# A planned attention and squared-relu kernel: a clock of transfers under way, and the values' maximum kept behind the relu passes of the second up product

## The chip, the core and the metric

The kernel runs on one core of a Trainium2 chip. The metric is device time in microseconds, the median of several executions; lower is better. The core has TensorE (PE in the profile; its weight loads are PEld), VectorE (DVE), ScalarE (ACT), GpSimd (POOL) and SyncE (SP). Each runs its own list of instructions in order and waits on semaphores for the others. Transfers are issued from the lists of POOL, SP and ACT.

## The reference

```python
# q: (8, 16, 384, 64); k, v: (8, 4, 384, 64); w_in: (1024, 2048); w_out: (2048, 1024)
k = np.repeat(k, 4, axis=1); v = np.repeat(v, 4, axis=1)
scores = np.matmul(q, k.transpose(0, 1, 3, 2)) / np.sqrt(64)
attn = np.exp(scores - np.max(scores, axis=-1, keepdims=True))
attn = attn / (np.sum(attn, axis=-1, keepdims=True) + 1e-09)
x = np.matmul(attn, v).transpose(0, 2, 1, 3).reshape(3072, 1024)
h = np.maximum(x @ w_in, 0.0)
return (h * h @ w_out).astype(np.float32)
```

Inputs and output are float32. Each of the 8 batches gives 384 rows of `x`.

## The kernel before

**Stages.** A batch `b` passes through loads of q, k and v (POOL queue, cast to bf16), transposes of k and q by DMA (SP queue; `turn_k_half`, `turn_q_dma`), scores on TensorE with the exponential on ScalarE (L476), the product with the values (`av_halves`, L533) with the division on VectorE (L546, L548), a transpose of the result into `xT` by DMA (`turn_o_dma`, L553), the up product with `w_in`, the relu and the square, and the down product with `w_out`, whose results are stored from the tiles `y_sb` (L1329).

**Up and down products.** For batches 0 and 1 the up product is done in quads (`quad`): four tiles of 128 columns in banks 4 to 7 of PSUM, in phases; VectorE takes the relu of a phase out of two banks (L642) before TensorE may fill them again. From batch 2 on, both products are of Strassen's kind: seven products of sums of quarters. The sums of the input are made on VectorE (`sums`, L676, a queue named `lazy`, whose last entry, L679, marks the batch as summed; only then is its up product offered). `strassen` puts units of the up product into the four banks of `order`, and the down products follow in the same banks. VectorE and ScalarE evict each down product into a y tile (L1114, L1115, L1121); for product 7 GpSimd adds two y tiles (L1153), and product 4 is then evicted into one of the tiles that this pass reads.

**Scales.** The kernel works in scaled 16-bit numbers. The largest value of `v` in a batch is reduced on VectorE (`top_of`, L691 and L693), spread over the partitions by TensorE (`top_spread`, L703, L707), and made into a unit (`v_unit`, L712) before attention of that batch may start. It waits in a queue `top_q`. In the second up product (batch 1) VectorE also scales `w_out` in place, pass by pass (`here2`, L1247), whenever its clock is near that of TensorE.

**Order of the work.** Nothing of the order is written out by hand. `Recorder` keeps a clock for every engine, with a cost for every operation. Two loops choose, step by step, the next piece for TensorE by the time at which its inputs are ready by these clocks; before each step `upkeep(now)` hands passes to the other engines from queues, by conditions on the clocks. `emit` then writes each engine's list with the waits. A change of a cost or a condition therefore moves the order of much that comes after it.

**Transfers.** From batch 2 on, `calm_at` decides whether a load or a transpose may be issued. It works from the number of TensorE instructions recorded so far: TensorE's instructions are fetched in blocks, and a block is taken as 128 matmuls with an offset `EDGE`. Where TensorE issues 18 or more matmuls per us, a transfer may start if the next edge is at least 1.5 us away and the last one 0.3 us past. `dma_at` keeps a gap of 2.0 us after a load and 3.5 us after a transpose. This applies to the loads and the transposes of k and q from batch 4 on, and to the transposes of attention's output in the second loop.

Of the kernel before, what the change touches and what calls it, by code (L numbers as in the profile page):

```python
# [21 lines left out]
class Recorder:  # L22


    ENGINES = ("tensor", "scalar", "vector", "gpsimd", "sync")
    IN_ORDER = ("tensor",)

    def __init__(self, nc):
        self.nc = nc
        self.ops = []  # L30
        self.writer = {}
        self.readers = {}
        self.dma_sems = {}
# [27 lines left out]
    def add(self, eng, fn, reads=(), writes=(), dma=None, cost=0.1, issue=0.1, shared=(), after=(), port=False):  # L61
# [19 lines left out]
        start = max([self.clock[eng]] + [self.ops[d]["end"] for d in need])  # L81
        if dma is not None:
# [7 lines left out]
            if shared and self.ring.get("gpsimd", 0.0) > begin:  # L90
# [76 lines left out]
def bass_gqa_attention__then__ffn_squared_relu_kernel(  # L167
# [17 lines left out]
    NKC = F // 128  # L185
# [1140 lines left out]
    def send(b, i3, c0, c1, yb, y0=0):  # L1326
        ysl = y_sb[yb][:, y0:y0 + c1 - c0]
        rows = out[b * S:(b + 1) * S, :].rearrange("(p j) f -> j p f", j=NJ)[i3]
        put = lambda: R.add("sync", lambda e: e.dma_start(rows[:, c0:c1], ysl),  # L1329
                            reads=[("y", yb)], writes=[("out", b, i3, c0)], dma=f"y{yb}" + "z" * (y0 > 0), cost=0.6)  # L1330
# [108 lines left out]
    def prepare(b):  # L1439
# [218 lines left out]
    o_wait = []  # L1658

    def turn_o_waiting():  # L1660
        while o_wait:
            b, g = o_wait.pop(0)
            turn_o_dma(b, g, tuple(pe_last))
            dma_at[0] = max(dma_at[0], R.clock["tensor"] + 3.5)
            x_done[b] += 2

    def upkeep(now):
        nonlocal loaded, queued, turned
        pe_last[0:1] = [len(R.ops) - 1 - next(i for i, o in enumerate(reversed(R.ops)) if o["eng"] == "tensor")]
        if o_wait and calm_at(now):  # L1670
            turn_o_waiting()
        if loaded + 1 < B and turned >= loaded and not turn_q and not load_pieces and not chores:
# [17 lines left out]
            else:  # L1690
# [3 lines left out]
                if n < LATE:  # L1694
                    load_pieces.append(([("v_st", 0)], lambda g: load_v(n, g)))
        if load_pieces and now >= dma_at[0] and calm_at(now) and R.when(writes=load_pieces[0][0], reads=(load_pieces[0] + ((),))[2], eng="none") + 2.0 <= now:
# [7 lines left out]
        stretch[0] = split and ff["b"] < SB or bool(ff["now"])  # L1704
        while chores and R.when(reads=chores[0][0], eng="none") + (chores[0] + (False, 0.0))[3 if len(chores[0]) > 3 else -1] <= now + margin and not (len(chores[0]) > 2 and chores[0][2] and (now < dma_at[0] or not calm_at(now))):
            chores.pop(0)[1]()
            if not chores and not halves:
                turned = queued
# [17 lines left out]
        if m_q and not spread_q and (not ff["now"] or R.clock["vector"] <= now) and not (wide_q and wide_q[0][0] <= m_q[0][0]) and R.clock["vector"] <= now + 0.6:  # L1726
            m_q.pop(0)[1]()
        if top_q and (not spread_q or queued >= LATE) and top_q[0][2]() and (ff["b"] < SB or not ff["now"] or queued >= LATE) and R.when(reads=top_q[0][0], eng="none") + (4 if queued < LATE else 0.0) <= now + margin:
            top_q.pop(0)[1]()
# [286 lines left out]
```

## Time and profile before

| | us |
|---|---|
| median of 3 runs | 399.15 (398.44 to 399.24) |
| the profiled execution | 397.95 |
| its span | 396.0 |
| TensorE busy | 388.1 (98%) |
| VectorE busy | 316.3 (80%) |
| ScalarE busy | 264.4 (67%) |
| GpSimd busy | 151.1 (38%) |

The granted clock of TensorE is 1.00 throughout. Roughly, by the instructions on TensorE: the opening and batches 0 and 1 up to 125 us; the up products of batches 2 to 7 from about 128, 168, 222, 259, 313 and 348 us, each followed by its down product; the last matmul ends at about 392.8 us and the last store lands at 395.6 us.

A row of the timeline gives start, duration, engine, line, operation, tiles written and read, shapes, count, and in brackets the idle time of the engine before it with what ended it. A row of waits gives who waited for whom, the total, how often, and the longest. A row of windows gives the stretch, its length, the busy time of PE, PEld, DVE, ACT and POOL, the clock, the share of DMA and GB/s. A row by line and tile gives the count, the shortest, median and longest duration in ns, and the first and last start. "q" behind an engine is its sequencer. Ends of matmuls are modelled.

### The profile page before, as it was taken

Reading aid. Unit: us, or ns where it says so; the run is one execution under the profiler, and the core shown is the slowest. Engines: PE = TensorE matmul, PEld = TensorE weight load, DVE = VectorE, ACT = ScalarE, POOL = GpSimd, SP = SyncE. Lnnn points to the kernel's source line nnn. Section 1 sums busy time; section 2 is a strip of 40 time slices with the busy share of each in tenths; the row PEclk is TensorE's granted clock in tenths of the full one; section 3 lists DMA queues with packets and bytes.
Section 4 is the critical chain, followed back from the end, with each engine's and each line's share of the span. In section 5 each row is a group of like instructions: output and inputs, shape, how many; then the busy total and the mean of one; then the engine's idle time right before and its main releaser. Section 6 shows DMA issues by size and latency. Waiting matters only on the chain.

```text
span 396.0 us, 15645 instructions
## 1 busy us (share of the span) xinstructions
PE 388.1 (98%) x7022; PEld 292.1 (74%) x7022; DVE 316.3 (80%) x654; ACT 264.4 (67%) x384; POOL 151.1 (38%) x173
## 2 busy tenths in 40 slices
PE   8999999999999999999999999999999999999996
PEld 5565764455655998499876899799974799789653
DVE  3689879899989998878997888878897688856642
ACT  6948999688556796578728587868725597426511
POOL 8656410056002565068413263066420145126111
PEclk9999999999999999999999999999999999999999
DMA  9999999995229936659469957484476221120022
GB/s 171 175 199 187 207 186 192 180 221 82 41 77 141 163 49 83 109 123 102 64 112 190 139 89 73 89 149 58 65 107 167 79 45 25 46 84 3 28 81 106
DMA packets 95634, 44.39 MB, mean 112 GB/s; under 512 B 75984, under 2 KB 89552, under 8 KB 95568
## 3 DMA queue, kind: packets, MB, share of 16 engines
q0 software_dynamic: 36672, 17.44, 35.4%
q1 hardware_dynamic: 58224, 25.47, 32.1%
q8 instruction: 55, 0.90, 0.9%
q10 hardware_dynamic: 672, 0.49, 0.4%
q14 instruction: 11, 0.09, 0.1%
HBM read 35.65 MB, written 12.58 MB: 122 GB/s over the span
## 4 chain that ended last, share of the span: by engine, by line
PE 87%; DVE 7%; DMA 3%; POOL 1%; issue 1%; ACT 0%; ACTq 0%; DVEq 0%
PE ps L963 30%; PE ps L921 27%; PE ps L629 7%; PE ps L466 7%; PE ps L533 7%; PE ps L1297 5%; DMA wx<-in_q_dram 2%; PE ps L492 2%; DVE hr L642 1%; PE ps L592 1%; DMA wx<-in_k_dram 1%; DVE w_out_sb L1247 1%; DVE y_sb L1121 1%; DVE w_out_sb L1259 1%; DVE s_all L676 0%
## 5 line engine op out<-in xcount | busy, mean ns | idle before, releaser
L476 ACT ACTIVATE expT<-ps 128x1024 bf16<-128x1024 f32 (+1 forms) x124 | 121.1, 1017 | 37.6 <-PE ps L466 37.2
L963 PE MATMUL ps<-w_out_sb,h2T 64*128 64x512 f16 x528 | 96.3, 376 | 0.0
L921 PE MATMUL ps<-xT,w_in_sb 64*128 64x192 f16 x1152 | 84.2, 243 | 0.4 <-DVE y_sb L1121 0.3
L921 PEld LDWEIGHTS ps<-xT,w_in_sb 64*128 64x128 f16 x1152 | 71.4, 94 | 3.4 <-DVE y_sb L1121 0.5
L818 POOL TENSOR_TENSOR h2T<-hr 128x384 f16<-128x384 f32 x56 | 45.4, 832 | 45.6 <-ACT hr L806 45.4
L963 PE MATMUL ps<-area,xT 64*128 64x512 f16 x288 | 55.3, 376 | 0.0
L963 PEld LDWEIGHTS ps<-w_out_sb,h2T 64*128 64x128 f16 (+1 forms) x528 | 38.5, 94 | 19.0 <-ACT h2T L814 0.5
L921 PE MATMUL ps<-s_all,wx 64*128 64x192 f16 x768 | 51.8, 243 | 0.0
L466 PE MATMUL ps<-qT,kT 64*128 64x256 bf16 (+2 forms) x336 | 50.3, 323 | 0.9 <-ACT expT L476 0.6
L806 ACT ACTIVATE hr<-hr,bits 128x384 f32<-128x384 f32 x71 | 41.9, 608 | 10.1 <-DVE hr L905 9.5
L921 PEld LDWEIGHTS ps<-s_all,wx 64*128 64x128 f16 x768 | 44.4, 94 | 0.7
L905 DVE TENSOR_TENSOR hr<-ps,hr 128x384 f32<-128x384 f32 x72 | 39.2, 554 | 6.3 <-PE ps L921 2.5
L533 PE MATMUL ps<-v_aug,expT 64*128 64x65 bf16 x1680 | 43.9, 190 | 0.1
L1121 DVE SCALAR_TENSOR_TENSOR y_sb<-ps,bits,y_sb 128x512 f32<-128x512 f32 (+2 forms) x38 | 27.1, 723 | 20.4 <-PE ps L963 9.6
L629 PE MATMUL ps<-xT,w_in_sb 64*128 64x384 bf16 x448 | 41.9, 323 | 1.0 <-DVE hr L642 0.9
L533 PEld LDWEIGHTS ps<-v_aug,expT 64*128 64x128 bf16 x1680 | 39.9, 94 | 1.4 <-PE ps L533 0.2
L1114 ACT ACTIVATE y_sb<-ps,bits 128x512 f32<-128x512 f32 x20 | 13.6, 687 | 35.4 <-PE ps L963 35.4
L963 PE MATMUL ps<-area,h2T 64*128 64x512 f16 x144 | 36.2, 376 | 0.0
L1153 POOL TENSOR_TENSOR y_sb<-y_sb 128x512 f32<-128x512 f32 x9 | 11.9, 1320 | 62.7 <-DVE y_sb L1121 62.7
L629 PEld LDWEIGHTS ps<-xT,w_in_sb 64*128 64x128 bf16 x448 | 21.9, 94 | 16.2 <-DVE hr L642 2.2
L921 PE MATMUL ps<-xT,wx 64*128 64x192 f16 x384 | 33.0, 243 | 0.2 <-DVE hr L905 0.2
L921 PE MATMUL ps<-s_all,w_in_sb 64*128 64x192 f16 x384 | 32.7, 242 | 0.0
(147 smaller groups left out, 748.5 us busy)
## 6 DMA issues: line engine op xcount, KB each, us to landing
out_dram<-y_sb SPq DMA_DIRECT2D x45, 256.0 KB, 2.5
w_in_sb<-in_moe_w_in_dram POOLq DMA_DIRECT2D x8, 512.0 KB, 15.2
w_out_sb<-in_moe_w_out_dram POOLq DMA_DIRECT2D x4, 1024.0 KB, 28.4
q_st<-in_q_dram POOLq DMA_DIRECT2D x19, 192.0 KB, 4.9
q_st<-in_q_dram POOLq DMA_DIRECT2D x4, 384.0 KB, 23.5
k_st<-in_k_dram POOLq DMA_DIRECT2D x6, 192.0 KB, 4.5
k_st<-in_v_dram POOLq DMA_DIRECT2D x5, 192.0 KB, 3.8
wx<-in_q_dram POOLq DMA_DIRECT2D x2, 384.0 KB, 9.1
```

The costliest lines, as they stand in the source:

```text
L466: mm = pe.matmul(ps[:, base + x, m * wide:(m + 1) * wide], kT[at(b)][64 * x:64 * x + 64, u, :], q_cols(b, u // NJ, x, c0, c0 + wide))
L476: R.add("scalar", lambda e: e.activation(dst, src, AF.Exp, scale=0.125), reads=keys, writes=[("expT", slot(b, u), t) for u, _, _ in pieces ...
L533: m = pe.matmul(ps[:, p[x], n * DP:n * DP + D + 1], w, v_aug[b % 2][r, g * NJ + j, 0:D + 1], start=(n + j + y == 0), stop=(n + j + y == 2 ...
L629: m = pe.matmul(bank(4 + xs[x])[:, 0:S], w_in_sb[r, kc, c * 128:(c + 1) * 128], xT[b % NXT][r, kc, :], start=(phase < 2 and kc == 0), stop ...
L806: R.add("scalar", lambda e, val=val, to=to: e.activation(val, val, AF.Relu, scale=to), reads=[("hr", r)] + by, writes=[("hr", r)], cost=0. ...
L818: n = R.add(eng, lambda e, dst=dst, two=two: e.tensor_tensor(dst, two, two, ALU.mult), reads=[("hr", r)], writes=keys, cost=0.77 if other ...
L905: R.add("vector", lambda e: e.tensor_tensor(hr[r][:, :], src, hr[r][:, :], ALU.add), reads=[("bank", at), ("hr", r)], writes=[("hr", r)], ...
L921: return lambda pe: pe.matmul(bank(at)[:, f * h:f * h + h], w[r, kc, c:c + 128], m[r, kc, :], start=(prod in (1, 5, 2) and y + f + kc == 0 ...
L963: return lambda pe: pe.matmul(bank(p.at)[:, 0:512], p.a(k, r), p.w(k, r), start=start, stop=stop, skip_group_check=True)
L1114: R.add(eng, lambda e: e.activation(y_sb[y], bank(at), AF.Copy, scale=gs[g]) if eng == "scalar" else e.tensor_scalar(y_sb[y], bank(at), gs ...
L1121: R.add("vector", lambda e: e.scalar_tensor_tensor(y_sb[z][:, c0:c1], bank(at)[:, c0:c1], gs[g], y_sb[y][:, c0:c1], ALU.mult, ALU.add), re ...
L1297: m = pe.matmul(bank(i)[:, 0:n], h2T[:, c, i3 * 128:(i3 + 1) * 128], w_out_sb[:, c, c0:c1], start=(c == 0), stop=(c == NFC - 1))
```

## The change

- A clock of transfers: every transfer that is recorded adds to `wire`, with a lag and a duration by kind. `calm_at` now asks, by kind, whether the transfers under way with the new one would be over within 6 us (where TensorE issues under 18 matmuls per us), or within 2 us past the next edge, or whether an edge is at most 0.3 us away and what is under way ends within 2 us.
- The gaps behind a load and a transpose become 0.5 us from batch 2 on, and the gap of 3.5 us behind the transpose of an attention output becomes 0.
- `shut`: from batch 2 on, a pass of `lazy` isn't handed to VectorE while, at the later of the two clocks, a GpSimd operation is under way in the plan with over 0.3 us left.
- `top_q` isn't served in the second up and down product (`ff["b"] == 1`) while VectorE's clock is over 0.3 us past TensorE's.
- The last batch's products use banks 0 to 3 in place of 4 to 7.
- The store of the second piece of the last tile (`y0` not 0) is issued from ScalarE's list in place of SyncE's.
- A bound in front of `add_sums` is written with one case more, of the same value.

```diff
+    WIRE = dict(turn_q=(1.6, 1.9), turn_o=(0.8, 1.3), turn_k=(1.3, 1.3), y=(1.8, 0.8))
...
+        self.wire = 0.0
...
             self.ring[q] = begin + cost
+            kind = dma.rstrip("0123456789z_")
+            lag, work = self.WIRE.get(kind, (2.2, 1.25))
+            self.wire = max(self.wire, start + lag) + work
...
-        put = lambda: R.add("sync", lambda e: e.dma_start(rows[:, c0:c1], ysl),
+        put = lambda: R.add("scalar" if y0 else "sync", lambda e: e.dma_start(rows[:, c0:c1], ysl),
...
-                dma_at[0] = R.clock["tensor"] + TURN_GAP
+                dma_at[0] = R.clock["tensor"] + (TURN_GAP if ff["b"] < SB else 0.5)
...
+            if b == B - 1:
+                order[:] = [0, 1, 2, 3]
             built[b] = strassen(b, ff["carry"])
...
-    def calm_at(now):
+    def calm_at(now, kind):
...
         rate = (n - m) / (now - t)
+        lag, work = R.WIRE.get(kind, (2.2, 1.25))
+        over = max(R.wire, now + lag) + work
         if rate < 18:
-            return True
+            return over <= now + 6.0
         left = (EDGE - n) % BLOCK / rate
-        return 1.5 <= left <= BLOCK / rate - 0.3
+        return (over <= now + left + 2.0 or left < 0.3 and R.wire <= now + 2.0) and left <= BLOCK / rate - 0.3
...
-            dma_at[0] = max(dma_at[0], R.clock["tensor"] + 3.5)
+            dma_at[0] = max(dma_at[0], R.clock["tensor"] + 0)
...
+    def shut(now):
+        t = max(now, R.clock["vector"])
+        return ff["b"] >= SB and any(a <= t < z - 0.3 for a, z in R.pool[-6:])
...
-            dma_at[0] = now + LOAD_GAP
+            dma_at[0] = now + (LOAD_GAP if ff["b"] < SB else 0.5)
...
-        while lazy and R.when(reads=lazy[0][0], eng="none") <= now + near and R.clock["vector"] <= now + near:
+        while lazy and R.when(reads=lazy[0][0], eng="none") <= now + near and R.clock["vector"] <= now + near and not shut(now):
             lazy.pop(0)[1]()
...
-        if top_q and (...) and R.when(reads=top_q[0][0], eng="none") + (4 if queued < LATE else 0.0) <= now + margin:
+        if top_q and (...) and R.when(reads=top_q[0][0], eng="none") + (4 if queued < LATE else 0.0) <= now + margin and not (ff["b"] == 1 and R.clock["vector"] > now + 0.3):
             top_q.pop(0)[1]()
...
-        if b and R.when(reads=[("xT", b % NXT, c) for c in range(NKC)], eng="none") + (3.3 if b > SB else 2.0) <= now + 0.3:
+        if b and R.when(reads=[("xT", b % NXT, c) for c in range(NKC)], eng="none") + (3.3 if b > SB + 1 else 3.3 if b > SB else 2.0) <= now + 0.3:
             add_sums(b)
```

The calls of `calm_at` pass the kind: `"turn_o"` for attention's output, `"q"` for loads, `"turn_q"` for the transposes of k and q.

More of the change, by code (lines that the diff above doesn't have):

```diff
@@ L1669, in upkeep @@
         pe_last[0:1] = [len(R.ops) - 1 - next(i for i, o in enumerate(reversed(R.ops)) if o["eng"] == "tensor")]
-        if o_wait and calm_at(now):
+        if o_wait and calm_at(now, "turn_o"):
             turn_o_waiting()
@@ L1695, in upkeep @@
                     load_pieces.append(([("v_st", 0)], lambda g: load_v(n, g)))
-        if load_pieces and now >= dma_at[0] and calm_at(now) and R.when(writes=load_pieces[0][0], reads=(load_pieces[0] + ((),))[2], eng="none") + 2.0 <= now:
+        if load_pieces and now >= dma_at[0] and calm_at(now, "q") and R.when(writes=load_pieces[0][0], reads=(load_pieces[0] + ((),))[2], eng="none") + 2.0 <= now:
             load_pieces.pop(0)[1](tuple(pe_last[0:1]))
-            dma_at[0] = now + LOAD_GAP
+            dma_at[0] = now + (LOAD_GAP if ff["b"] < SB else 0.5)
         if not chores and halves and (halves[0] - 1, NU - 1, 5) in scored and (halves[0] > LATE or x_done[halves[0] - 1] == NKC):
@@ L1704, in upkeep @@
         stretch[0] = split and ff["b"] < SB or bool(ff["now"])
-        while chores and R.when(reads=chores[0][0], eng="none") + (chores[0] + (False, 0.0))[3 if len(chores[0]) > 3 else -1] <= now + margin and not (len(chores[0]) > 2 and chores[0][2] and (now < dma_at[0] or not calm_at(now))):
+        while chores and R.when(reads=chores[0][0], eng="none") + (chores[0] + (False, 0.0))[3 if len(chores[0]) > 3 else -1] <= now + margin and not (len(chores[0]) > 2 and chores[0][2] and (now < dma_at[0] or not calm_at(now, "turn_q"))):
             chores.pop(0)[1]()
@@ L1727, in upkeep @@
             m_q.pop(0)[1]()
-        if top_q and (not spread_q or queued >= LATE) and top_q[0][2]() and (ff["b"] < SB or not ff["now"] or queued >= LATE) and R.when(reads=top_q[0][0], eng="none") + (4 if queued < LATE else 0.0) <= now + margin:
+        if top_q and (not spread_q or queued >= LATE) and top_q[0][2]() and (ff["b"] < SB or not ff["now"] or queued >= LATE) and R.when(reads=top_q[0][0], eng="none") + (4 if queued < LATE else 0.0) <= now + margin and not (ff["b"] == 1 and R.clock["vector"] > now + 0.3):
             top_q.pop(0)[1]()
```

## The prediction

> **What bounds the kernel now.** I read the page's busy shares and chain first, then TensorE's own waits, then the timeline around each wait, last the tail and the transfers.
>
> ```profile
> span 396.0 us, 15645 instructions
> PE 388.1 (98%) x7022; PEld 292.1 (74%) x7022; DVE 316.3 (80%) x654; ACT 264.4 (67%) x384; POOL 151.1 (38%) x173
> PE 87%; DVE 7%; DMA 3%; POOL 1%; issue 1%; ACT 0%; ACTq 0%; DVEq 0%
> PE ps L629 <- DVE hr L642: 0.9, 2, 0.7
> PE ps L963 <- DVE y_sb L1121: 0.6, 1, 0.6
> PE ps L466 <- ACT expT L476: 0.6, 3, 0.3
> PE ps L921 <- DVE y_sb L1121: 0.3, 1, 0.3
> ```
>
> TensorE is busy 98% of the span and is 87% of the chain, so only what makes TensorE wait, and the tail after its last matmul, can be won. Its waits (total, times, longest) are short and few: the four rows give 2.4 us, and VectorE, evicting late, is behind 1.8 of them. The 7% of VectorE in the chain are these places. So I go through the change by what it does to them.
>
> **The change, part by part.** *The values' maximum behind the relu passes (the new condition on `top_q` while `ff["b"] == 1`).* VectorE, then TensorE, at the place of the longest wait:
>
> ```profile
> 80.86 0.17 DVE L1244 RECIPROCAL bits<-bits 128x1 f32<-128x1 f32 x1
> 80.94 0.93 DVE L691 TENSOR_REDUCE bits<-area 128x1 f32<-128x768 bf16 x1
> 81.91 0.23 DVE L693 CAST top_w<-bits 128x128 bf16<-128x128 f32 x1
> 82.06 1.01 DVE L642 TENSOR_SCALAR hr<-ps 128x384 f32<-128x384 f32 x2
> 82.99 2.63 DVE L1247 TENSOR_SCALAR w_out_sb<-w_out_sb,bits 128x1024 f16<-128x1024 bf16 x5
> ...
> 80.71 0.65 PE L629 MATMUL ps<-xT,w_in_sb 64*128 64x384 bf16 x6
> 81.63 0.81 PE L629 MATMUL ps<-xT,w_in_sb 64*128 64x384 bf16 x8
> 83.13 0.34 PE L629 MATMUL ps<-xT,w_in_sb 64*128 64x384 bf16 x2 [0.68 <-DVE hr L642]
> ```
>
> The maximum and its cast (0.93 + 0.23 us) stand ahead of two relu passes. The phase whose banks they empty ended at 80.71 + 0.65 = 81.36. Without the maximum the pair would run from there to 81.36 + 1.01 = 82.37, and TensorE's other work lasts to 81.63 + 0.81 = 82.44. The whole wait goes: 0.68 us. On the chip VectorE has no gap between the passes up to here; the planner's VectorE clock, which follows the same passes, is then past `now + 0.3`, and the condition bites. The maximum isn't removed: it runs behind the pair, among the scale passes of L1247, which only have to be done before the down product from about 101 us. That is its cover: about 18 us. If it lands ahead of a later relu pair instead, it costs up to the same 0.68; range 0 to 0.68, taken 0.68, because the room of 2.63 us behind the pair holds its 1.16.
>
> *`shut`: no sum on VectorE while the plan has a GpSimd pass under way.* VectorE, GpSimd, TensorE in the down product of batch 5, then the groups of both operations:
>
> ```profile
> 295.96 0.54 DVE L676 TENSOR_TENSOR xT<-xT 128x768 f16<-128x768 f16 x1
> 296.42 1.62 DVE L676 TENSOR_TENSOR s_all<-xT,s_all 128x768 f16<-128x768 f16 x1
> 297.97 0.74 DVE L1121 SCALAR_TENSOR_TENSOR y_sb<-ps,bits,y_sb 128x512 f32<-128x512 f32 x1
> ...
> 296.12 1.51 POOL L1153 TENSOR_TENSOR y_sb<-y_sb 128x512 f32<-128x512 f32 x1 [2.83 <-DVE y_sb L1121]
> ...
> 298.76 0.39 PE L963 MATMUL ps<-w_out_sb,area 64*128 64x512 f16 x1 [0.63 <-DVE y_sb L1121]
> ...
> L676 DVE TENSOR_TENSOR s_all<-xT,s_all x6: 548/550/1621, 126.4 to 345.0; 128x768 f16<-128x768 f16 x6
> L1153 POOL TENSOR_TENSOR y_sb<-y_sb x9: 1256/1268/1507, 167.6 to 391.3; 128x512 f32<-128x512 f32 x9
> ```
>
> The sum takes 1.62 us beside the GpSimd pass and 0.55 in the median; the pass ends at 296.12 + 1.51 = 297.63, and the sum 0.4 us behind it. Moved away from the pass, the sum frees VectorE for 1.62 - 0.55 = 1.07 us.
>
> TensorE does not get that much. The eviction of L1121 at 297.97 writes the y tile that the GpSimd pass reads (product 7's `a3`, product 4's target), so it waits for that pass too: alone it would end at 296.12 + 1.27 = 297.39, the eviction at 298.13, TensorE would start at 298.18 and not 298.76. That is 0.58. Late next are the two sums, 0.54 + 0.55 us, which now stand between later evictions; their reader, the up product of batch 6, starts 15 us on. Bounds 0 (the sums make the next eviction late by as much) and 0.63 (the wait's row); taken 0.5, nearer the upper, since TensorE's other evictions here show no wait. For the other batches the guard delays a sum by less than one GpSimd pass, hidden by the same distance, but for one place (second rival).
>
> *Banks 0 to 3 for the last batch (`order[:]`).* At its start TensorE meets the last evictions of batch 6 in banks 4 to 7:
>
> ```profile
> 348.97 0.89 PE L921 MATMUL ps<-xT,w_in_sb 64*128 64x192 f16 x10
> 350.14 0.34 PE L921 MATMUL ps<-xT,w_in_sb 64*128 64x192 f16 x4 [0.28 <-DVE y_sb L1121]
> ...
> 349.33 1.41 DVE L1121 SCALAR_TENSOR_TENSOR y_sb<-ps,bits,y_sb 128x512 f32<-128x512 f32 x2 [1.46 <-PE ps L921]
> ```
>
> Scores and attention are over by then, so banks 0 to 3 are free and this wait has no cause left: 0.28 us by its row. Ends of matmuls are modelled, so the real stop may be some 0.1 longer. Bounds 0 (VectorE, whose two evictions still take 1.41 us, is late for the first evictions of the new product instead) and 0.4; taken 0.3, by the row: VectorE had idled 1.46 us before these two and has room.
>
> *The last piece of the output on ScalarE's queue.* SP, the last two stores, and the second alone, with their times to landing:
>
> ```profile
> 393.45 0.82 SPq L1329 DMA_DIRECT2D out_dram<-y_sb  x2
> 393.83 0.45 SPq L1329 DMA_DIRECT2D out_dram<-y_sb  x1
> DMA to landing us min/median/max: 1.8/1.8/1.9
> ```
>
> Both wait for the same VectorE pass. The first lands at 393.45 + 1.9 = 395.35, the second at 393.83 + 1.8 = 395.6. From another queue the second starts up to 0.38 sooner, and then the first sets the end: 0.25 at best, 0 if the two slow each other. Taken 0.2; ScalarE has nothing left to do behind it.
>
> *The clock of transfers (`WIRE`, `calm_at`, the shorter gaps).* No transfer is added; those of batches 4 to 7 (five loads of q and k and one of v, four transposes each) and the transposes of attention's output start at other moments, mostly sooner, since 2.0 and 3.5 us between them become 0.5 and 0. Two stretches of the same up product, with many transfers and with few, and the instruction queue:
>
> ```profile
> 222.00:246.00 24.00, 24.00 (x707) 23.52 (x701) 20.48 (x45) 18.99 (x30) 11.06 (x13) 1.00 0.73 106
> 313.00:337.00 24.00, 24.00 (x720) 23.56 (x714) 20.48 (x46) 18.76 (x30) 9.55 (x11) 1.00 0.26 61
> q8 instruction: 55, 0.90, 0.9%
> ```
>
> With DMA at 0.73 and at 0.26 TensorE is busy all 24.00 us and VectorE 20.48, so spaced transfers cost nothing now and there is nothing to win by spacing them better. The 55 instruction blocks take 0.009 x 16 x 396 / 55 = 1.04 us each and no wait of TensorE is put down to them. POOL and SP issue them as before; POOL has 62% of the span free for what queues behind a load. A gain isn't excluded: scores could come earlier and take ScalarE's 0.6 us (first table) off TensorE. A loss neither, as bundles of transfers do not occur in this trace. I take 0, between +0.6 and the loss of the third rival. [...]
>
> The new bound for `add_sums` has the same 3.3 on both sides: no change.
>
> **Sum.** 0.68 + 0.5 + 0.3 + 0.2 = 1.68, say 1.7 us. The profiled execution took 397.95 (span 396.0 and 1.95 around it), so 396.25; the median of the runs is 399.15, 1.2 above the profiled one, so the forecast against it is 399.15 - 1.7 = 397.45.
>
> **The rivals.** *Transfers sooner also help:* 0.6 us of waits on ScalarE go too, 396.85; against it, ScalarE is idle a third of the span, so more room won't bring its passes earlier by itself.
>
> *`shut` holds back what the third batch needs.* ScalarE, GpSimd, VectorE and TensorE as the up product of batch 3 opens:
>
> ```profile
> 166.81 2.85 ACT L476 ACTIVATE expT<-ps 128x1024 bf16<-128x1024 f32 x3 [0.95 <-PE ps L466]
> 167.58 1.51 POOL L1153 TENSOR_TENSOR y_sb<-y_sb 128x512 f32<-128x512 f32 x1 [10.83 <-DVE y_sb L1121]
> 167.88 0.21 DVE L679 TENSOR_SCALAR bits<-bits 128x1 f32<-128x1 f32 x1
> 168.12 0.24 PE L921 MATMUL ps<-xT,w_in_sb 64*128 64x192 f16 x1
> ```
>
> The last entry of the queue that `shut` guards is L679, and without it the batch is not marked as summed, so its first piece isn't offered. Here it lies inside a GpSimd pass. Held back, the planner would choose scores, whose banks are emptied by the second exp pass, at 166.81 + 2 x 0.95 = 168.71: TensorE waits from 168.12, 0.6 us. The time is 398.05. For it: the pass is there; against: a shift of half a us takes L679 out of it.
>
> *Slower: bundled transfers make TensorE wait.* Four batches (4 to 7) have all their loads and transposes under the new clock. If a bundle delays an instruction block or a transpose of attention's output by enough for one wait as long as the longest seen, about 0.7 us, each of them loses that. Three waits (2.1) eat the 1.7; with one for each batch, four, it is 399.15 - 1.7 + 2.8 = 400.25. The break-even is between two and three. For it: in the stretch of 0.73 the queues are already near full in places. Against: nothing shows a wait on a transfer after the opening.
>
> *The edits do not bite:* the planner's clock and the chip drift apart, the maximum and the sums stand before other passes of the same kind, and only banks and tail are won, paid back by one new wait of 0.6: 399.15 or so.
>
> **How the numbers follow.** Forecast 0.45, transfers help 0.12, the third batch 0.15, bundles 0.17, no bite 0.11. A measurement can tell about 0.2%, 0.8 us, from no change: faster means below 398.35, slower above 399.95. The forecast, the first rival and four fifths of the second are faster: 0.45 + 0.12 + 0.12 = 0.69; the rest of the second and the fourth are the same: 0.14; bundles are slower: 0.17. Time 397.45. Range 395.4 to 400.4: the top holds the four-wait case of the bundles, the bottom is the first rival with every upper bound (0.68 + 0.63 + 0.4 + 0.25 + 0.6 = 2.56 us, 396.6) and about one us for the shifts of small waits that a new plan brings, of which four rows of 2.4 us in all give the size. For the faster cases alone it is 395.6 to 398.3.
>
> **What would show it.** In the waits of TensorE: no row of L629 behind L642 as long as 0.7, no L963 behind L1121 of 0.6, none of L921 behind L1121 near the start of the last batch. In groups: the longest sum of L676 near 0.55 and not 1.62. In the tail: the last store on ScalarE's queue, landing within 0.1 us of the 192 KB before it. In the windows: TensorE still 24.00 of 24.00 in the up products. What would make it wrong: TensorE waiting on ScalarE or on its sequencer in the up products, or a new wait on VectorE of the size of those removed.

## The result and the profile after

| | before | changed |
|---|---|---|
| median of 6 runs, us | 398.88 (398.0 to 400.0) | 394.75 (394.15 to 395.47) |
| the profiled execution, us | 397.95 | 395.19 |
| its span, us | 396.0 | 393.4 |

The changed kernel is faster: ratio 0.9897, 95% interval 0.9877 to 0.9916, some 4.1 us or 1%. The prediction had the direction and 1.7 us; the measured time lies below its range. In the changed kernel L629 has become L634, L676 L681, L921 L926, L963 L968, L1121 L1126, L1153 L1158 and L1329 L1334.

The page's span, its row of busy times and TensorE's waits (line, whom it waited for, total, times, longest), after:

```profile
span 393.4 us, 15642 instructions
PE 387.3 (98%) x7019; PEld 302.6 (77%) x7022; DVE 308.3 (78%) x646; ACT 272.2 (69%) x397; POOL 144.6 (37%) x168
...
PE ps L1389 <- PEq L2014: 0.8, 1, 0.8
PE ps L634 <- DMA w_in_sb<-in_moe_w_in_dram: 0.4, 1, 0.4
PE ps L471 <- ACT expT L481: 0.4, 2, 0.2
PE ps L398 <- ACT k_dup L1397: 0.3, 1, 0.3
PE ps L926 <- DVE y_sb L1126: 0.2, 1, 0.2
PE ps L634 <- DVE hr L647: 0.2, 1, 0.2
```

The waits of 0.7, 0.6 and 0.3 us that the prediction aimed at are no longer there. The wait of 0.8 on TensorE's own sequencer is there in both kernels, and one wait of 0.4 on the transfer that loads `w_in` stands in the opening, at 37 us. The timeline at the three places, and where the third batch opens (VectorE's sums of L681 and GpSimd's passes behind them):

```profile
80.31 1.47 PE L634 MATMUL ps<-xT,w_in_sb 64*128 64x384 bf16 x16
82.05 2.11 PE L634 MATMUL ps<-xT,w_in_sb 64*128 64x384 bf16 x24
...
81.36 1.00 DVE L647 TENSOR_SCALAR hr<-ps 128x384 f32<-128x384 f32 x2
82.28 0.48 DVE L1252 TENSOR_SCALAR w_out_sb<-w_out_sb,bits 128x1024 f16<-128x1024 bf16 x1
82.68 0.94 DVE L696 TENSOR_REDUCE bits<-area 128x1 f32<-128x768 bf16 x1
...
163.50 0.55 DVE L681 TENSOR_TENSOR s_all<-xT 128x768 f16<-128x768 f16 x1
...
165.03 0.55 DVE L681 TENSOR_TENSOR s_all<-xT,s_all 128x768 f16<-128x768 f16 x1
...
166.61 1.25 POOL L1158 TENSOR_TENSOR y_sb<-y_sb 128x512 f32<-128x512 f32 x1 [1.12 <-DVE y_sb L1126]
167.82 1.88 POOL L1225 COPY area<-h2T 128x2048 f16<-128x2048 f16 x1
...
296.22 0.55 DVE L681 TENSOR_TENSOR s_all<-xT,s_all 128x768 f16<-128x768 f16 x1
...
296.38 1.51 POOL L1158 TENSOR_TENSOR y_sb<-y_sb 128x512 f32<-128x512 f32 x1 [13.32 <-DVE y_sb L1126]
...
346.74 2.21 PE L926 MATMUL ps<-xT,w_in_sb 64*128 64x192 f16 x42
```

The relu pair starts at 81.36, where the prediction put it, the maximum stands behind it at 82.68, and TensorE goes on without a stop. The sum at 296.22 takes 0.55 us and not 1.62. At the start of the last batch 42 matmuls of L926 run through. The third batch's sums run from 163.50 to 165.58, clear of the GpSimd passes from 166.61 on; nothing in the prediction says that this place matters, and it is what the experiments turn on.

The tail of the timeline (VectorE's last pass and the two last stores), and from the view of the output tile the times of these two to landing:

```profile
389.67 1.07 DVE L1126 SCALAR_TENSOR_TENSOR y_sb<-ps,bits,y_sb 128x384 f32<-128x384 f32 x2 [0.24 <-PE ps L1023]
...
390.77 0.33 SPq L1334 DMA_DIRECT2D out_dram<-y_sb  x1
390.77 0.37 ACTq L1334 DMA_DIRECT2D out_dram<-y_sb  x1
```

```profile
DMA to landing us min/median/max: 2.0/2.1/2.2
```

Both stores now start together, and they take 2.0 us (SP) and 2.2 us (ScalarE) to land instead of 1.8 to 1.9. From the first issue to the end of the span it is 393.4 - 390.77 = 2.63 us; before it was 396.0 - 393.45 = 2.55.

### The profile page after: what moved, and what is told of

Same layout as the page of the kernel before. It is cut to its first block, busy times and chain, and to the rows that moved or that the text cites. A ratio compares the mean times of both kernels' runs of the same rounds, so it can differ in the third digit from the quotient of the medians.

```text
span 393.4 us, 15642 instructions
## 1 busy us (share of the span) xinstructions
PE 387.3 (98%) x7019; PEld 302.6 (77%) x7022; DVE 308.3 (78%) x646; ACT 272.2 (69%) x397; POOL 144.6 (37%) x168
## 5 line engine op out<-in xcount | busy, mean ns | idle before, releaser
L968 PE MATMUL ps<-w_out_sb,h2T 64*128 64x512 f16 x528 | 98.0, 376 | 0.0
L926 PE MATMUL ps<-xT,w_in_sb 64*128 64x192 f16 x1152 | 84.4, 243 | 0.3 <-DVE y_sb L1126 0.2
L926 PEld LDWEIGHTS ps<-xT,w_in_sb 64*128 64x128 f16 x1152 | 70.7, 94 | 3.0 <-PE ps L926 0.7
L968 PE MATMUL ps<-area,xT 64*128 64x512 f16 x288 | 55.7, 376 | 0.0
L926 PE MATMUL ps<-s_all,wx 64*128 64x192 f16 x768 | 52.0, 242 | 0.0
L471 PE MATMUL ps<-qT,kT 64*128 64x256 bf16 (+2 forms) x336 | 51.1, 326 | 0.5 <-ACT expT L481 0.4
L968 PEld LDWEIGHTS ps<-w_out_sb,h2T 64*128 64x128 f16 (+1 forms) x528 | 38.9, 94 | 16.1 <-ACT h2T L819 0.3
L1126 DVE SCALAR_TENSOR_TENSOR y_sb<-ps,bits,y_sb 128x512 f32<-128x512 f32 (+2 forms) x38 | 27.1, 725 | 24.1 <-PE ps L968 14.1
L926 PEld LDWEIGHTS ps<-s_all,wx 64*128 64x128 f16 x768 | 44.0, 94 | 1.2
L538 PE MATMUL ps<-v_aug,expT 64*128 64x65 bf16 x1680 | 42.5, 190 | 0.1
L634 PE MATMUL ps<-xT,w_in_sb 64*128 64x384 bf16 x448 | 41.6, 323 | 0.6 <-DMA w_in_sb<-in_moe_w_in_dram 0.4
L1119 ACT ACTIVATE y_sb<-ps,bits 128x512 f32<-128x512 f32 x23 | 15.6, 687 | 36.9 <-PE ps L968 36.7
L538 PEld LDWEIGHTS ps<-v_aug,expT 64*128 64x128 bf16 x1680 | 39.0, 94 | 2.0 <-DVE o_sb L553 0.3
L1158 POOL TENSOR_TENSOR y_sb<-y_sb 128x512 f32<-128x512 f32 x9 | 11.6, 1290 | 65.7 <-DVE y_sb L1126 65.7
L968 PE MATMUL ps<-area,h2T 64*128 64x512 f16 x144 | 35.6, 376 | 0.0
L634 PEld LDWEIGHTS ps<-xT,w_in_sb 64*128 64x128 bf16 x448 | 22.1, 94 | 15.2 <-issue 1.5
L926 PE MATMUL ps<-xT,wx 64*128 64x192 f16 x384 | 32.5, 242 | 0.0
L926 PE MATMUL ps<-s_all,w_in_sb 64*128 64x192 f16 x384 | 32.4, 242 | 0.0
```

The costliest lines, as they stand in the source:

```text
L471: mm = pe.matmul(ps[:, base + x, m * wide:(m + 1) * wide], kT[at(b)][64 * x:64 * x + 64, u, :], q_cols(b, u // NJ, x, c0, c0 + wide))
L538: m = pe.matmul(ps[:, p[x], n * DP:n * DP + D + 1], w, v_aug[b % 2][r, g * NJ + j, 0:D + 1], start=(n + j + y == 0), stop=(n + j + y == 2 ...
L634: m = pe.matmul(bank(4 + xs[x])[:, 0:S], w_in_sb[r, kc, c * 128:(c + 1) * 128], xT[b % NXT][r, kc, :], start=(phase < 2 and kc == 0), stop ...
L926: return lambda pe: pe.matmul(bank(at)[:, f * h:f * h + h], w[r, kc, c:c + 128], m[r, kc, :], start=(prod in (1, 5, 2) and y + f + kc == 0 ...
L968: return lambda pe: pe.matmul(bank(p.at)[:, 0:512], p.a(k, r), p.w(k, r), start=start, stop=stop, skip_group_check=True)
L1119: R.add(eng, lambda e: e.activation(y_sb[y], bank(at), AF.Copy, scale=gs[g]) if eng == "scalar" else e.tensor_scalar(y_sb[y], bank(at), gs ...
```

## The experiments

Each run is compared with runs of the kernel before on the same chip. "Difference" is median minus the median of before. The medians of the kernel before lie between 398.07 and 398.88 us on the chips, so differences between kernels measured on different chips are uncertain by about 0.8 us, those on one chip by less (e1 to e4, e5 to e8, and e9 to e15 shared a chip each).

| kernel | parts of the change in it | us | ratio, 95% interval | difference |
|---|---|---|---|---|
| changed | clock, shut, banks, store, maximum | 394.75 | 0.9897, 0.9877 to 0.9916 | -4.1 |
| e1 | clock | 403.01 | 1.0111, 1.0087 to 1.0136 | +4.9 |
| e2 | maximum | 397.14 | 0.9965, 0.9952 to 0.9977 | -0.9 |
| e3 | shut | 399.56 | 1.0028, 1.001 to 1.0045 | +1.5 |
| e4 | banks | 397.46 | 0.9984, 0.9968 to 1.0 | -0.6 |
| e5 | all but the maximum | 401.49 | 1.0084, 1.0061 to 1.0108 | +3.4 |
| e6 | all but the clock | 396.29 | 0.9953, 0.9932 to 0.9974 | -1.8 |
| e7 | all but shut | 394.47 | 0.9906, 0.9884 to 0.9928 | -3.6 |
| e8 | clock, maximum | 395.31 | 0.9926, 0.9906 to 0.9945 | -2.8 |
| e9 | as e6, small loads | 394.78 | 0.9897, 0.988 to 0.9915 | -3.7 |
| e10 | as changed, small loads | 393.93 | 0.9878, 0.9858 to 0.9898 | -4.6 |
| e11 | changed, transfers never held | 399.57 | 1.0024, 1.0012 to 1.0036 | +1.1 |
| e12 | as e5, one pass moved | 400.29 | 1.0035, 1.0016 to 1.0055 | +1.8 |
| e13 | before, small loads | 397.34 | 0.996, 0.9942 to 0.9978 | -1.2 |
| e14 | as e6, and the clock's test | 395.88 | 0.9933, 0.9911 to 0.9955 | -2.7 |
| e15 | as e6, and the clock's gaps | 399.88 | 1.0034, 1.0012 to 1.0057 | +1.3 |

### The parts one by one

e1 is the kernel before with the clock of transfers alone: `WIRE`, `wire`, the new `calm_at` and its calls, and

```diff
-                dma_at[0] = R.clock["tensor"] + TURN_GAP
+                dma_at[0] = R.clock["tensor"] + (TURN_GAP if ff["b"] < SB else 0.5)
...
-            dma_at[0] = max(dma_at[0], R.clock["tensor"] + 3.5)
+            dma_at[0] = max(dma_at[0], R.clock["tensor"] + 0)
...
-            dma_at[0] = now + LOAD_GAP
+            dma_at[0] = now + (LOAD_GAP if ff["b"] < SB else 0.5)
```

> The kernel before with the clock of transfers alone (WIRE, calm_at, the shorter gaps). My prediction's terms: 0, so 398.9 against 398.9 before, within 0.5. Rival (the part that was not priced carries the rest of the gain): 4.1 measured less the 1.7 of the other parts, 2.4 us faster, 396.5. Second rival (nothing belongs to one part, the waits move with every new order): anything within 1 us of before, and the parts don't add up.

It is 4.9 us slower, which none of the three expectations allowed. Its trace has a wait of 3.76 us at the opening of the third batch, as long as in e5, whose rows stand below:

```profile
175.29 2.14 PE L926 MATMUL ps<-xT,w_in_sb 64*128 64x192 f16 x32 [3.76 <-DVE y_sb L1126]
```

e2 has the maximum's condition alone:

```diff
-        ... + (4 if queued < LATE else 0.0) <= now + margin:
+        ... + (4 if queued < LATE else 0.0) <= now + margin and not (ff["b"] == 1 and R.clock["vector"] > now + 0.3):
```

> The kernel before with the condition on the values' maximum alone. By the prediction 0.68 us faster, 398.2, and no wait of TensorE on the relu of 0.7 us in the second up product. If the clock carries the gain: the same 0.7. If the waits move with every new order: the wait of 0.7 goes, others come or go, between 397.5 and 399.5.

0.9 us faster (0.9 to 1.9 by the interval), where the prediction's term was 0.68. The two waits of L629 behind L642, 0.68 at 83.13 us and 0.26 at 94.21, were 0.9 together; both are gone, and one of 0.2 at 88 us is new. The profiled execution of e2 (397.52, the highest of its runs) has a stop that is put down to nothing in the trace. The timeline, the windows around it, and the transfers of 262.0 to 267.3 us and of 267.3 to 268.6 us by queue (packets, MB, share):

```profile
269.90 0.25 PE L921 MATMUL ps<-xT,wx 64*128 64x192 f16 x1 [1.24 <-issue]
```

```profile
269.00:270.00 1.00, 0.10 (x4) 0.10 (x6) 0.19 (x1) 0.92 (x2) 1.00 (x2) 1.00 0.08 7
```

```profile
q1 hardware_dynamic: 978, 0.65, 77.1%
q0 software_dynamic: 906, 0.34, 53.8%
...
q0 software_dynamic: 458, 0.17, 120.3%
q8 instruction: 1, 0.02, 5.7%
```

For 5.3 us no instruction block came in, and for the first 3.8 of them the queues of loads, stores and transposes were full (a DMA share of 1.22 from 262 to 264 and of 2.07 from 264 to 266). The next block set out just after 267.3, with a load under way, and TensorE stopped from 268.66 to 269.90. A late block is possible, but the trace doesn't show it: from 265.8 to 267.0 the DMA engines had little to do (a share of 0.09 from 266 to 267) and no block came in then either. So the row shows a stop of 1.24 us and leaves its cause open.

e3 has `shut` alone:

```diff
-        while lazy and ... and R.clock["vector"] <= now + near:
+        while lazy and ... and R.clock["vector"] <= now + near and not shut(now):
```

> The kernel before with the guard on the sums alone (shut). By the prediction 0.5 us faster, 398.4: the sum of 1.62 us becomes 0.55 and the wait of 0.63 in the down product of batch 5 goes. If the guard holds back the third batch's opening (the prediction's second rival): a wait of 0.6 at about 168 us and no gain, 399.

1.5 us slower. The timeline of e3 at the third batch's opening:

```profile
166.68 3.77 ACT L476 ACTIVATE expT<-ps 128x1024 bf16<-128x1024 f32 x4 [0.95 <-PE ps L466]
...
167.46 1.51 POOL L1153 TENSOR_TENSOR y_sb<-y_sb 128x512 f32<-128x512 f32 x1 [10.84 <-DVE y_sb L1121]
...
167.76 0.21 DVE L679 TENSOR_SCALAR bits<-bits 128x1 f32<-128x1 f32 x1
...
168.68 0.39 PE L466 MATMUL ps<-qT,kT 64*128 64x512 bf16 x2 [0.52 <-ACT expT L476]
```

This is the prediction's second rival to the letter: the planner chose scores, and TensorE waits for the second exp pass until 168.68 (the rival said 168.71), 0.52 us. On the chip the entry L679 itself ran inside the GpSimd pass; it is the plan that held the batch back. In the same profile three waits of TensorE are put down to nothing in the trace: L921 twice, 0.5 us together, and L533 once, 0.4. In batch 5 the guard did what was expected of it: the longest sum takes 0.56 us, and the wait of 0.63 there is gone. So the profile shows 0.5 and 0.9 us of new waits against 0.6 won, with one new wait of 0.3 behind L1201; the rest of the 1.5 us isn't accounted for.

e4 has the banks alone:

```diff
         if b not in built:
+            if b == B - 1:
+                order[:] = [0, 1, 2, 3]
```

> The kernel before with banks 0 to 3 for the last batch alone. The order of the work up to 348 us stays. By the prediction 0.3 us faster, 398.6, and no wait on L1121 as the last up product opens. If the gain belongs to the clock: the same 0.3.

0.6 us faster, with an interval that reaches no change; the term was 0.3. The wait of L921 at the last batch is gone.

### What the parts do to each other

e1 to e4 add up to +4.9, and the whole change, which adds only the store, is -4.1. So kernels followed that leave out one part, and one with the two parts of the title.

> The changed kernel without the condition on the values' maximum (clock, guard, banks and store kept). If the parts add up: 0.9 us slower than the changed kernel, as the condition alone gave 0.9 against before, so 395.7. If the clock and the condition act together (the clock alone lost 4.9 us at one place, the opening of the third batch, where the sums met GpSimd's copy of k; with the condition all later work is recorded sooner and that meeting does not occur): the wait of some 3.8 us is back, about 402.

> The changed kernel without the clock of transfers and the shorter gaps. If the parts add up, the clock costs 4.9 us and this is 4.9 faster than the changed kernel, 389.9. If the clock is worth something only together with the condition: between the sum of maximum and banks, 396.5, and 398, slower than the changed kernel by 2 to 3 us, with waits of TensorE put down to its own issue (instruction blocks late) and one at the third batch's opening.

> The changed kernel without the guard on the sums. TensorE's list is the same as in the changed kernel, only some passes on VectorE and GpSimd stand in another order in one down product. If the guard matters only there: 0 to 0.7 us slower, 394.8 to 395.4. If the guard is what keeps the third batch's sums off GpSimd: a wait of 3 us or more, 398.

> The kernel before with the clock and the condition on the maximum, nothing else. If these two act together: 395.3 to 396, most of the gain, with 0.3 to 0.6 for the banks still missing. If the parts add up: 398.07 + 4.9 - 0.9 = 402.

The theory that the clock and the maximum act together held in e5 and e8. e6 came 0.2 under its second range, without the waits on TensorE's own issue that were expected; e7 came below both of its ranges.

With the clock in the kernel, the maximum's condition is worth 401.49 - 394.75 = 6.7 us and not 0.7 (7.5 if each is taken against before on its own chip). The clock and the maximum alone have 2.8 of the 4.1 us. Without the clock the other four parts win 1.8. No gain of `shut` is shown beside the clock: 394.47 without it, 394.75 with it, or 0.5 us in its favour by the differences, which is within what chips differ by.

The timeline of e5 at the third batch's opening, on VectorE, GpSimd and TensorE, and then its windows (length, busy time of PE, PEld, DVE, ACT and POOL, granted clock, DMA share, GB/s):

```profile
167.49 1.23 DVE L681 TENSOR_TENSOR s_all<-xT 128x768 f16<-128x768 f16 x1
168.76 2.13 DVE L681 TENSOR_TENSOR s_all<-s_all,xT 128x768 f16<-128x768 f16 x1
170.81 1.81 DVE L681 TENSOR_TENSOR xT<-xT 128x768 f16<-128x768 f16 x1
172.54 0.55 DVE L681 TENSOR_TENSOR s_all<-xT,s_all 128x768 f16<-128x768 f16 x1
...
167.05 1.26 POOL L1158 TENSOR_TENSOR y_sb<-y_sb 128x512 f32<-128x512 f32 x1
168.26 2.21 POOL L1225 COPY area<-h2T 128x2048 f16<-128x2048 f16 x1
170.42 1.79 POOL L361 COPY k_dup<-k_st 128x1536 bf16<-128x1536 bf16 x1
...
174.48 1.78 PE L926 MATMUL ps<-xT,w_in_sb 64*128 64x192 f16 x20 [3.76 <-DVE y_sb L1126]
```

```profile
173.00:174.00 1.00, 0.00 (x0) 0.00 (x0) 0.93 (x5) 0.00 (x0) 0.00 (x0) 0.69 0.00 0
...
175.00:176.00 1.00, 1.00 (x16) 0.93 (x14) 0.93 (x5) 0.48 (x1) 0.00 (x0) 0.50 0.00 0
...
179.00:180.00 1.00, 1.00 (x12) 0.71 (x10) 0.00 (x0) 0.53 (x1) 0.00 (x0) 0.50 1.00 373
180.00:181.00 1.00, 1.00 (x38) 0.97 (x36) 0.66 (x2) 1.00 (x3) 0.00 (x0) 0.90 0.28 105
```

Here the sums come 4 us later than in the changed kernel (167.49 against 163.50), and three of the four run beside a GpSimd pass. Each starts while a GpSimd pass is under way and ends 0.4 us behind the end of that pass (at 168.31, 170.47 and 172.21): 1.23, 2.13 and 1.81 us in place of 0.55. The order of the starts matters: in the changed kernel the sum at 296.22 started 0.16 us ahead of its pass and took 0.55; there the pass took 1.51 us where it takes 1.25 alone. The three take 3.5 us longer than they need, VectorE's next evictions come after them, and TensorE stops 3.76 us. Then comes a second loss: the granted clock falls to 0.50 towards the end of the stop (0.69 in the window of 173) and stays there until about 180.2, with TensorE at work again from 174.48. That is 5.7 us at half speed, by estimate 2.9 us more. So 3.76 + 2.9 = 6.6 us, beside 0.7 for the relu wait that is back, against 402.99 - 395.19 = 7.8 between the two profiled executions. This execution is one of two with a mean clock of 0.991; the other four have 0.995 or 0.996, by estimate from these means about half as long at half speed, so in them the stop, up to 1.7 us for the clock and 0.7 make up to 6.2 of the 6.7 us.

e12 takes one of the three passes away. It is e5 with the copy of k for batch 5 on ScalarE:

```diff
-        eng = "scalar" if b > 1 and not stretch[0] else "gpsimd"
+        eng = "scalar" if b > 1 and (b == 5 or not stretch[0]) else "gpsimd"
```

> The four parts without the maximum's condition (401.49 us), with one pass moved: the copy of k of batch 5 (1.79 us on GpSimd at 170.42, beside the third of the sums that open the third batch) runs on ScalarE; the lists of TensorE, VectorE and SyncE are the same. Theory (each GpSimd pass keeps VectorE's sum waiting): the third sum falls from 1.81 to 0.55 us, the first two stay at 1.2 and 2.1 beside the two y passes, TensorE's wait of 3.8 there falls to about 2.5, and the time to 400.2 +- 0.4. Rival (the sums are slow by something else, such as the transfers that bunch there under the clock): the third sum stays near 1.8 us and the time near 401.5.

400.29, as the theory had it. (The second of the two passes that are left is the copy of L1225, not a y pass.) The timeline of e12 and one of its windows:

```profile
168.23 2.13 DVE L681 TENSOR_TENSOR s_all<-s_all,xT 128x768 f16<-128x768 f16 x1
170.28 0.55 DVE L681 TENSOR_TENSOR xT<-xT 128x768 f16<-128x768 f16 x1
...
172.69 1.49 PE L926 MATMUL ps<-xT,w_in_sb 64*128 64x192 f16 x32 [2.50 <-DVE y_sb L1126]
```

```profile
174.00:175.00 1.00, 1.00 (x42) 1.00 (x38) 0.97 (x3) 0.38 (x1) 0.00 (x0) 1.00 0.00 0
```

The third sum is back at 0.55 us and the wait down from 3.76 to 2.50, by the 1.26 that this sum lost. So it was the GpSimd pass beside it that made this sum long, 1.81 us in e5. In this execution the clock stayed at 1.00, and its time, 398.46, is among the lowest. The 12 runs of e12 tell the price of the clock by itself: the four with a mean granted clock of 1.00 took 398.35 to 398.97 us, the seven with 0.995 or 0.996 took 400.15 to 401.69 (one with 0.999 took 399.85). By estimate a mean of 0.996 over 398 us is 1.6 us lost.

### What the clock of transfers wins

On top of the other four parts the clock wins 396.29 - 394.75 = 1.5 us, or 2.3 if each is taken against before on its own chip. The trace of e6 has no wait of TensorE over 0.3 us but one of 0.8 on its own sequencer, which before and changed have too, so a trace of waits can't tell where this comes from. Its profiled execution, 395.55, is also the shortest of its eight. The next kernels cut the loads of batches 4 to 7 to 8 values of one head per partition; most of their data is left out, and the order of all work stays. The lines for k (q and v alike):

```diff
-            k_st[st].rearrange("p (g j) d -> p g (j d)", j=NJ),
-            k[b].rearrange("g (p j) d -> p g (j d)", j=NJ)),
+            k_st[st].rearrange("p (g j) d -> p g (j d)", j=NJ)[:, 0:1 if b > SB + 1 else HKV, 0:8 if b > SB + 1 else NJ * D],
+            k[b].rearrange("g (p j) d -> p g (j d)", j=NJ)[:, 0:1 if b > SB + 1 else HKV, 0:8 if b > SB + 1 else NJ * D]),
```

e9 is e6 with these, e10 the changed kernel, e13 the kernel before.

> The four other parts without the clock of transfers, with the loads of q, k and v for batches 4 to 7 cut to 8 values of one head per partition; the plan and every engine's order are those of the kernel without the clock (396.29 us, runs from 395.55 to 397.66). The loads leave most of their data out, so attention of these batches works on what is left in the tiles. Theory: what the clock still wins (396.29 to 394.75) is the traffic of loads that makes instruction blocks, and with them TensorE, late; with nearly no load traffic this kernel comes to 394.6 +- 0.5 and its runs lie within 1.3 us, with no wait of TensorE on its sequencer over 0.4 us. Rival: the clock wins by another order of the passes; then the time stays at 396.3 +- 0.5 and the spread at 2 us.

> The changed kernel with the same loads cut to 8 values of one head per partition, leaving the rest of their data out; plan and order as in the changed kernel. Theory: the clock already keeps its loads from making TensorE late, so little is left to win: 394.5, between 394.0 and 394.9. Rival: transfers still cost TensorE something in the changed kernel, by ports or by late blocks: 393.7 or less.

> The kernel before with the loads of q, k and v for batches 4 to 7 cut to 8 values of one head per partition, leaving the rest of their data out. Theory: load traffic costs this order of transfers what it cost the kernel without the clock, 396.29 - 394.78 = 1.5 us, so 396.6 to 397.0, and the runs lie within 1 us. Rival: the traffic costs nothing as in the prediction, and the loss without the clock was another one; then 398.1 to 398.5, runs 2 us apart.

e9 came to 394.78, 1.5 us under e6, with runs from 394.36 to 394.97 where those of e6 lay 2.1 us apart. So load traffic costs the order without the clock 1.5 us (1.9 against before on each chip), although no wait in its trace shows it. e10 came to 393.93, just under what the theory allowed: by the medians the changed kernel still pays 0.4 to 0.8 us for loads. Its trace can't place them: matched by their starts, the matmuls of the changed kernel's profiled execution lie 1.3 us behind those of e10 at the end, but 0.95 of that arises by 38 us, before the first load that is cut (at 117 us), and only 0.35 behind it, at 258 us. e13 came to 397.34, between its two expectations: before pays 1.2 us for loads, but its runs stay 2.4 us apart, so loads aren't all that makes them differ. With small loads 394.78 - 393.93 = 0.85 us are left between e9 and e10; that part of the clock's gain isn't the bulk of the loads. What is left is the order and the moments of the work (transposes and stores included); these weren't told apart.

e11 takes the test of the moment away and leaves the short gaps:

```diff
-            return over <= now + 6.0
+            return True
...
-        return (over <= now + left + 2.0 or ...) and left <= BLOCK / rate - 0.3
+        return True or (over <= now + left + 2.0 or ...) and left <= BLOCK / rate - 0.3
```

> The changed kernel with the test of the transfers' moment answering yes always: gaps of 0.5 and 0 us stay, nothing is kept from an edge or behind what is under way. Theory (bundles that meet the instruction blocks stop TensorE): 396.5 to 398.5, with waits of TensorE on its sequencer in the profile, and a spread of 2 us or more; the plan itself has one new wait on VectorE of 0.56 us at the third batch's opening. Rival (the moment of a transfer is worth nothing, only the shorter gaps and the order count): 394.75 + 0.56 = 395.3, spread as in the changed kernel.

399.57, slower than either expected, and for another reason than either gave. No wait on TensorE's sequencer is new. The third batch's sums start at 166.44 instead of 163.50, two of them meet the GpSimd passes (1.51 and 2.24 us), and the 0.56 us of the plan became a stop of 2.5 us. The timeline of e11 on VectorE, GpSimd and TensorE, and its windows:

```profile
167.02 1.51 DVE L681 TENSOR_TENSOR s_all<-s_all,xT 128x768 f16<-128x768 f16 x1
168.45 2.24 DVE L681 TENSOR_TENSOR xT<-xT 128x768 f16<-128x768 f16 x1
...
166.60 1.51 POOL L1158 TENSOR_TENSOR y_sb<-y_sb 128x512 f32<-128x512 f32 x1 [2.08 <-DVE y_sb L1126]
168.07 2.21 POOL L1225 COPY area<-h2T 128x2048 f16<-128x2048 f16 x1
...
172.56 2.00 PE L926 MATMUL ps<-xT,w_in_sb 64*128 64x192 f16 x32 [2.48 <-DVE y_sb L1126]
```

```profile
173.00:174.00 1.00, 1.00 (x22) 0.93 (x18) 0.93 (x5) 0.53 (x2) 0.51 (x1) 0.69 0.00 0
...
176.00:177.00 1.00, 1.00 (x16) 0.72 (x12) 0.25 (x1) 0.20 (x1) 0.00 (x0) 0.60 1.49 212
```

The clock is at one half from about 173.4 to 176.8, 3.4 us, which by estimate costs half of that, 1.7. It falls 0.8 us after TensorE is at work again, at 172.56. So 2.5 + 1.7 = 4.2 of the 4.8 us are accounted for.

e14 and e15 split the clock of transfers on top of the other four parts. e14 has `WIRE` and `calm_at` with the old gaps; e15 has the three lines of gaps shown under e1, with the old `calm_at`.

> The four other parts, with the clock's test of the moment but the old gaps of 2.0 and 3.5 us. If the gain is the test of the moment (transfers kept clear of edges and of each other), 394.7 to 395.2, as in the changed kernel, with runs within 1.4 us. If it is the shorter gaps, which bring loads and transposes sooner, the time stays at 396.3 to 397, runs 2 us apart; the plan's own waits add up to about 0.6 us more than without the test.

> The four other parts with the shorter gaps, and the old test of the edge. The plan has a wait of 0.56 us at the third batch's opening, as in the kernel whose transfers were never held. If that meeting of the sums with GpSimd's passes repeats on the chip, TensorE stops 2.5 us there and its granted clock halves for 3.4 us behind it in most runs: 394.75 + 2.5 + 1.7 = 399 +- 0.6. If the passes miss each other, the gaps alone give the changed kernel's 394.7 to 395.3.

e14: 395.88, between its two expectations, with runs 2.3 us apart. e15: 399.88, with the stop of 2.5 us at the third batch's opening (its row of L921 behind L1121: total, times, longest), and 0.3 above the range that was expected for it.

```profile
PE ps L921 <- DVE y_sb L1121: 2.9, 2, 2.5
```

Its runs with a clock of 0.999 or more took 398.24 to 398.75, all but one of the others 399.69 to 401.75. Neither half carries the whole gain: the test alone is 0.4 us better than e6 by the medians and 0.9 by the differences, with intervals that overlap, and the gaps alone lose. With both, the third batch's sums stay clear of GpSimd's passes. These sums read what the last transpose of attention's output ahead of them writes. It is issued at 158.1 to 159.6 us in all five kernels with a stop of 2.5 us or more (e1, e5, e11, e12 and e15), and at 154.8 to 157.3 in the twelve others. So the stop goes with a late transpose; that the transpose alone causes it wasn't tested.

## Why the prediction was right in direction and wrong in size

- **The maximum, 0.68.** Right in place and mechanism: 0.9 alone, since a second wait of the same kind, 0.26 at 94.21 us, went with it. But it was priced in the plan of before. Beside the clock of transfers the same condition decides whether the third batch meets the GpSimd passes, and there it is worth 6.7.
- **`shut`, 0.5.** Wrong. The wait that it aimed at goes, but alone it costs 1.5 us; 0.5 of its new waits is the second rival, at the place and nearly the time predicted. In the changed kernel the sum is short without it as well (0.55 in e7). One sum of 1.99 us is left in spite of it, at 252 us, and costs TensorE no wait.
- **The banks, 0.3.** Right in mechanism: the wait is gone. The time is 0.6 lower alone, with an interval of 0 to 1.3 us that holds the term.
- **The store on ScalarE's queue, 0.2.** Wrong by the profiles (it was not run alone): 2.63 us from issue to the end against 2.55. This is the lower bound that the prediction named, "0 if the two slow each other".
- **The four together.** The prediction's sum of 1.7 is what e6 shows, 1.8, but that is partly luck: two of its terms are too small and two too large.
- **The clock of transfers, "I take 0".** This is the step that failed, "spaced transfers cost nothing now and there is nothing to win by spacing them better". It rested on TensorE being busy 24.00 of 24.00 us in two windows with a DMA share of 0.73 and 0.26. Ends of matmuls are modelled, so a window that is full by the profile needn't be a window in which TensorE lost nothing. What the runs showed in its place is 1.5 to 2.3 us on top of the other four parts; the 2.3, against before on each chip, and their 1.8 make the 4.1. e9 and e13 put the loads' cost at 1.2 to 1.9 us in the orders without the clock, where e10 puts it at 0.4 to 0.8 with it; 0.85 of the gain is left when the loads are cut. One sign stood in the prediction: the profiled execution was 1.2 us under the median, so the usual run lost time that this trace could not show, and the sum of waits left it out. That this was the loads isn't shown: with them cut, the runs of before still lie 2.4 us apart (e13).
- **Parts priced one by one.** The sum takes the clock and the maximum as independent. e1 and e8 show that they are not: the clock alone costs 4.9 us, with the maximum it wins.
- **A reading.** "The 7% of VectorE in the chain are these places" doesn't hold: 7% of 396 us is 28 us, and the waits behind VectorE are 1.8. No term rests on it.
- **The rivals.** "Transfers sooner also help" is what happened, but its 0.6 us was sized by the waits on ScalarE. "Bundles of transfers" came near in e1, e5, e11 and e15, in all of which the clock or half of it made the kernel slower; but by VectorE's sums meeting GpSimd, with one stop of 2.5 to 3.8 us, and not by four late blocks. The price of that rival, 2.8 us over four batches, is exceeded by one place.

What stays open: by what way load traffic costs TensorE time where no wait is shown (a stop like that of 1.24 us in e2 is one candidate), and why the plan with the clock hands out the third batch's sums 4 us later when the maximum isn't held back. 2.4 of the 4 us are there already at the transpose that the sums read (156.42 against 158.83), but not why it is issued later.

## What to carry to other kernels

Where a planner makes the order, the parts of a change don't add: price each part with and without the others, and look first at the places where two engines that disturb each other (here VectorE's 16-bit sums and GpSimd's passes: a sum of 0.55 us took 1.23 to 2.13 beside them in e5) are kept apart by a few us of chance. The stops of TensorE of 2.5 to 3.8 us here cost more than their length in most runs: the granted clock fell as well, to 0.50 for 3.4 us in the trace of e11, and its mean was 0.991 to 0.996 in 38 of the 48 runs of e1, e5, e11, e12 and e15. And the median of before, 399.15, lay 1.2 us above its profiled execution: the usual run lost time that the trace doesn't hold; leave room for it in the range.

## What the runs showed of the hardware

- A VectorE sum of 128x768 16-bit values that started while one of these GpSimd passes was under way ended 0.4 us behind that pass: in e5 0.55 us became 1.23, 2.13 and 1.81 beside passes of 1.26, 2.21 and 1.79. One pass taken away brought one sum back to 0.55 (e12). In the changed kernel a sum that started 0.16 us ahead of the pass kept its 0.55, and the pass took 1.51 us in place of 1.25.
- After a TensorE stop of 2.5 us the granted clock fell in most runs: the mean was 0.995 or 0.996 in 7 of 12 runs of e12 and 0.991 to 0.996 in 11 of 12 of e11, whose trace shows 0.50 for 3.4 us. With a stop of 3.76 us it fell in all runs of e1 and e5 (means of 0.991 to 0.996), to 0.50 for 6.8 us in the trace of e5. In e11 the stop was 2.48 us and TensorE had been at work again for 0.8 us when the clock fell; in e5 it fell 1.1 us before the end of the stop.
- The last two stores, of 192 and 64 KB, took 2.0 and 2.2 us to land when issued at the same moment from two queues, where one after the other on one queue they took 1.8 to 1.9; in these two executions the second queue won nothing.
